# Where the operands of a dense layer lie in on-chip memory, modulo 512 bytes: one gated attention-plus-SiLU kernel, with its buffers moved

## The chip, the cores and the metric

The kernel runs on one core of a Trainium2 chip. The metric is device time in microseconds (us) of one execution; shorter is better. On a core five engines work side by side, each through its own instruction stream: TensorE (PE in the profile, with its weight loads shown as PEld), VectorE (DVE), ScalarE (ACT), GpSimd (POOL) and SyncE (SP), which here issues the DMAs. They meet through semaphores. A matmul on TensorE reads two operands from the on-chip memory SBUF: the stationary one, loaded into the array by a weight load, and the moving one, streamed past it; the result goes to PSUM.

## What is computed

The reference mixes two branches of one input `x` (2048 tokens, 640 features), all in fp32:

```
g = sigmoid((x * gate_w).sum(-1, keepdims=True))
a = attention(x)              # 32 heads of 20; phi = softmax(q w_phi) and softmax(-q w_phi)
                              # o = phi_q (phi_k^T V) / (phi_q phi_k^T 1);  a = o @ wo
b = silu(x @ w1) @ w2         # w1: 640 x 1728, w2: 1728 x 640
out = g * a + (1 - g) * b
```

The attention is linear: `phi_k^T V` is summed over all tokens first, and then each query tile is multiplied by it.

## The kernel before: tiles, stages and names

**Split products.** Every large product is made of three matmuls in a fast fp32 format: an operand is split into a high and a low part (`split`, L117 to L120: ScalarE copies the high part, VectorE or GpSimd subtracts it), and the product takes high x high, high x low and low x high (`PASSES`). So each SBUF tile of an operand holds two halves, `[P, 2, ...]`, and with five chunks of 128 rows one output tile takes 5 x 3 = 15 matmuls.

**Stages**, in TensorE's order:

1. Keys and values (to about 190 us). For 16 token tiles, `kv_proj` (L460) multiplies `x` (tile `xa`, stationary) by the fused weights `wh` and `wl` (moving; a row of 1282 words for each of the five chunks, in pieces of 500, 500 and 282 columns). `kv_acc` (L430) and `kv_rest` (L441) sum `phi_k^T V`.
2. The dense part (to about 580 us). For four blocks of 512 tokens and 13 full tiles and one half tile of the 1728 features: `h_tile` (L507) makes `ph` from a `w1` tile (stationary) and the input tiles `xf` (moving, 512 columns), ScalarE takes the SiLU of it and splits it into a tile `u`; two tiles later `out_acc` (L688) adds `w2` tile (stationary) times `u` (moving, 512 columns) to five accumulators. The first block's first four `w1` products stand in `h_first` (L523).
3. Queries and output (from about 540 us, beside the end of stage 2). `proj` (L418) multiplies `x` (tile `xb` or `xf`, stationary) by `WQ` (moving, two halves of 320 columns), 15 matmuls for each half and 30 for a token tile; `t_mm` (L957) transposes, `n_mm` (L1031) applies `kvw`, and `w_mm` (L1074) applies the output weights `WO` (stationary) to `oT` (moving, 256 columns).

**Where the dense weights lie.** A tile pool lays tiles one behind the other in each partition. The dense weight tiles lie in four kinds of place, which keep their names in the profile:

- `w`, tiles of pool `fq` (`wslot`): the w1 tiles 0 to 4 and w2 tiles 0 to 3. A tile has 1280 words = 5120 bytes = 10 x 512.
- `f`: w2 tile 4, w1 and w2 tiles 5 to 8 and w1 tile 9 (ten tiles) lie as rows inside the two `big` buffers that held `wh` and `wl` before. `big_tile` has rows of `D + 2` = 642 words = 2568 bytes = 5 x 512 + 8, so each of these rows begins 8 bytes further round, modulo 512, than the row before it.
- `w` again, tiles of pool `fp`: w2 tile 9, and w1 and w2 tiles 10 to 12 (seven tiles of 5120 bytes).
- `w_r`: the half tile's weights (`W1R`, `W2R`), in pool `fp` too, with 10 matmuls in place of 15.

`WQ` and `WO` take the two `big` buffers after the `f` tiles. The tiles `xa`, `xf`, `xb` and `u` are slots of 4096 bytes = 8 x 512 (`slot`). The order of all work on each engine is written out by the program (`inorder` and the scheduler behind it).

Of the kernel before, what the change touches and what calls it, by code (L numbers as in the profile page):

```python
# [8 lines left out]
F32 = mybir.dt.float32  # L9
F32R = mybir.dt.float32r  # L10
# [6 lines left out]
P = 128  # L17
S = 2048
D = 640
H = 32  # L20
DH = 20
F = 1728
NC = D // P
NB = S // 512
NT = S // P
# [27 lines left out]
WC = 2 * D + 2  # L53
# [7 lines left out]
def mix_kernel(ctx: ExitStack, tc: tile.TileContext, xT, wqT, wkc, wkr, wv, bd, bdc, cst, wo, w1, w1r, w2, out):  # L61
    nc = tc.nc

    cp = ctx.enter_context(tc.tile_pool(name="cp", bufs=1))
    wp = ctx.enter_context(tc.tile_pool(name="wp", bufs=1))
# [3 lines left out]
    def opened(name, **kw):  # L69
        open_pools[name] = tc.tile_pool(name=name, bufs=1, **kw)  # L70
        return open_pools[name].__enter__()

    def closed(*names):
        for name in names:
            open_pools.pop(name).__exit__(None, None, None)

    fq = opened("fq")
    fu = opened("fu")
    ta = opened("ta")
    psk = opened("psk", space=PSUM)  # L80
    kvp = [psk.tile([P, 512], F32, name=f"kvp{k}") for k in range(3)]
# [14 lines left out]
        return ps.tile([P, 512], F32, tag=f"single{k % 4}", name=name, bufs=1)  # L96

    def raw(name):
        return wp.tile([P, D + 2], F32, tag="raw", name=name, bufs=4)

    def slot(name, pool=None, tag="x", bufs=7):
        return (pool or wp).tile([P, 2, 512], F32R, tag=tag, name=name, bufs=bufs)

    def big_tile(name):
        return wp.tile([P, 2, NC, D + 2], F32R, tag="big", name=name, bufs=2)

    def big(name):
        return big_tile(name).rearrange("p s c d -> p c s d")

    def big_kv(name):  # L110

        return big_tile(name).rearrange("p s c d -> p (s c d)")[:, : NC * WC].rearrange("p (c w) -> p c w", w=WC)

    def wslot(name, dt=F32):
        return fq.tile([P, 2 * D], dt, tag="w", name=name, bufs=NPRE)
# [26 lines left out]

    ident = cp.tile([P, P], F32, name="ident")
    make_identity(nc, ident)
    glog = cp.tile([P, NT], F32, name="glog")
    g = cp.tile([P, NT], F32, name="g")
    g1 = cp.tile([P, NT], F32, name="g1")
    stk = cp.tile([P, 4], F32, name="stk")
    warms = cp.tile([P, 1], F32, name="warms")
    ones = cp.tile([P, P], F32R, name="ones")  # L150
    stage = [ta.tile([P, 2, 2 * D], F32, tag="ph", name=f"stage{k}", bufs=2) for k in range(2)]
    stf = [t.rearrange("p a d -> p (a d)") for t in stage]
    st0 = [t[:, k * D : (k + 1) * D] for t in stf for k in range(3)][:NC]
# [42 lines left out]
    def x_of(t):  # L196
        return [x[:, :, t % 2 * P : (t % 2 + 1) * P] for x in X["t", t // 2]]
# [44 lines left out]
    held = {}  # L242

    def load_f(n):
        w, f = seq[n]
        k = n - NPRE
        if 0 <= k < 10:
            if k % 5 == 0:
                held[k // 5] = big(f"f{k // 5}")
            t = held[k // 5][:, k % 5, :, :D]  # L250
        else:
            t = wslot(f"w{w}_{f}", F32R).rearrange("p (s d) -> p s d", s=2) if n < NPRE else fp.tile([P, 2, D], F32R, name=f"w{w}_{f}")
        r = raw(f"wr{w}_{f}")
        src = w1[f] if w == 1 else w2[f * P : (f + 1) * P, :]
        nc.sync.dma_start(r[:, :D], src)
        split(t[:, 0, :], t[:, 1, :], r[:, :D], "pool" if n < NPRE else "dve")
        W[w, f] = t
# [29 lines left out]
    for k in range(WARM):  # L287
# [5 lines left out]
            stop=(k == WARM - 1),  # L293
        )

    WKV = [big_kv("wh"), big_kv("wl")]
    wh, wl = (w[:, :, :D] for w in WKV)
    LAST = D - NG * GW

# [15 lines left out]
    def kv_share(c, todo):  # L315

        for hx, hw in PASSES:
            for t, lo, hi, opens in todo:
                nc.tensor.matmul(  # L319
                    kv_cols(t, lo, hi),  # L320
                    x_of(t)[c][:, hx, :],
                    WKV[hw][:, c, lo:hi],
                    start=(opens and hx == 0 and hw == 0),
# [8 lines left out]
    def v_weights(c):  # L332
        r = ta.tile([P, 2 * D], F32, tag="e", name="wvr1", bufs=EB)[:, : D + 2] if c == 1 else flat(f"wvr{c}") if c == 2 else raw(f"wvr{c}")
        nc.sync.dma_start(r, wv[c * P : (c + 1) * P, :])
        split(WKV[0][:, c, D:], WKV[1][:, c, D:], r)

# [9 lines left out]
    with inorder(PE, ACT, DVE, POOL):  # L346
# [7 lines left out]
        for lo, hi in ((D, CUTS[2]), (CUTS[2], WC)):  # L354
            split(WKV[0][:, 0, lo:hi], WKV[1][:, 0, lo:hi], wv0[:, lo - D : hi - D])
        cols = [p for pair in zip(values(0), values(1)) for p in pair]
# [99 lines left out]
    def kv_proj(t, lo, hi):  # L456

        xt = x_of(t)
        for n, (hx, hw, c) in enumerate((hx, hw, c) for hx, hw in PASSES for c in range(NC)):
            nc.tensor.matmul(  # L460
                kv_cols(t, lo, hi),
                xt[c][:, hx, :],
                WKV[hw][:, c, lo:hi],
                start=(n == 0),
# [105 lines left out]
    with inorder(ACT, DVE, POOL):  # L570
        for t in range(NT - 1):
# [13 lines left out]
            mm = ta.tile([P, 2, H], F32, tag="mm", name=f"mmk{t}", bufs=2)  # L585
# [21 lines left out]
        t = NT - 1  # L607
# [8 lines left out]
        with inorder(PE):  # L616
# [7 lines left out]
            mm = ta.tile([P, 2, H], F32, tag="mm", name=f"mmk{t}", bufs=2)  # L624
# [48 lines left out]

    closed("psa", "psk", "ta")
    fp = opened("fp", reuse_waits="tile")
    ps = opened("psf", space=PSUM, reuse_waits="tile")

    def bank(name):
# [27 lines left out]
    nc.vector.tensor_tensor(W2R[:FR, 1, :], r[:FR, :D], W2R[:FR, 0, :].bitcast(F32), op=ALU.subtract)  # L706

    def load_wo():
        o = big("wo")
        for c in range(NG):  # L710
            r = raw(f"wo{c}")
            nc.sync.dma_start(r[:GW, :D], wo[c * GW : (c + 1) * GW, :])
            split(o[:GW, c, 0, :D], o[:GW, c, 1, :D], r[:GW, :D])
        return o
# [15 lines left out]
    def q_proj(t):  # L730
# [8 lines left out]
        for j in range(2):  # L739
            proj(dst[j], xq(t), WQ, j * HALF, HALF)  # L740
        return parts
# [2 lines left out]

    def q_open(t, parts):
        sm = fu.tile([P, 8 * H], F32, tag="sm", name=f"sm{t}", bufs=3)
        mm = fu.tile([P, 2, H], F32, tag="mmq", name=f"mmq{t}", bufs=2)
        sums.setdefault(t, sm[:, : 2 * H])
        e = wslot(f"eq{t}")
        Q[t] = {  # L750
            "e": e,
            "sm": sm,
            "mv": mm.rearrange("p i (a h) -> p i a h", a=2),
            "ev": e.rearrange("p (a h s f) -> p a h s f", a=2, s=2, f=DH),
            "parts": [(part, slice(k * 2 // len(parts), (k + 1) * 2 // len(parts))) for k, part in enumerate(parts)],
        }
# [121 lines left out]
    for b in range(NB):  # L878
        order = ORDERS[b]
        if b + 1 < NB:  # L880
            load_x("f", b + 1)
        acc = [bank(f"acc{b}_{m}") for m in range(NC)]
        us = {} if b else us0
        for n, f in enumerate(order):
            if f not in us:
                us[f] = h_tile(b, f)
            if n == 4:
                if b == 0:
                    pg = bank("pg")
                    nc.tensor.transpose(pg[:NT, :P], g1, ident)  # L890
                    gT = fp.tile([NT, P], F32, name="gT")
                    nc.scalar.copy(gT, pg[:NT, :P])
                    nc.sync.dma_start(g_d, gT)
                G1 = fp.tile([P, 512], F32, tag="G1", name=f"G1_{b}", bufs=1)
                nc.sync.dma_start(
                    G1, g_d.rearrange("t p -> (t p)")[b * 512 : (b + 1) * 512].partition_broadcast(P)
                )
            if n > 1 and n < NF:
                for m in range(NC):
                    out_acc(order, order[n - 2], us[order[n - 2]], acc, m)  # L900
            if b < NB - 1:
                continue
            if n == 2:
                load_b_consts()
            if n == 5:
                WQ = big("wq")
                zbc = wslot("zbc")
                nc.sync.dma_start(zbc, kv_d[KF].partition_broadcast(P))
            if 5 <= n < 5 + GR:
                gi = n - 5  # L910
                rq = raw(f"wTq{gi}")
                load_fused(gi, rq[:, :D])
                for c0, c1 in ((0, 4), (4, NC)):
                    fused(kvb["bd"], WQ[:, :, 0, :], WQ[:, :, 1, :], gi, rq, bank(f"pwq{gi}_{c0}"), c0, c1)
            if n == 8:
                WO = load_wo()
            if n == 9:
                kvw = [wslot(f"kvw{h}", F32R)[:GW, : 2 * NG * GW].rearrange("p (j f) -> p j f", f=GW) for h in range(2)]
                kvwr = fu.tile([RC, 2, GW], F32R, name="kvwr")
                make_kvw()  # L920
            if n == 8:
                xb_load(0)
                xb_split(0)
                xb_load(1)
                xb_split(1)
                xb_load(2)
            if 10 <= n < NF:
                t = 2 * NP - 4 + n - 10
                q_tile(t)
                if n < NF - 1:  # L930
                    q_rest(t)

        def acc_mm(m):
            for f in order[-3:]:
                out_acc(order, f, us[f], acc, m)

        def acc_out(m):
            o = fp.tile([P, 512], F32, tag="o", name=f"o{b}_{m}", bufs=2)
            nc.vector.tensor_tensor(o, acc[m], G1, op=ALU.mult)
            nc.sync.dma_start(fb_d[m, :, b * 512 : (b + 1) * 512], o)  # L940

        if b < NB - 1:
            for m in range(NC):
                acc_mm(m)
                acc_out(m)
# [33 lines left out]
    t = 2 * NP - 1  # L979
# [33 lines left out]
    tb = opened("tb", reuse_waits="tile")  # L1013
# [266 lines left out]
    with inorder(PE, DVE, ACT, POOL):  # L1280
# [15 lines left out]
        for u in range(1, NP - 2):  # L1296
            step(u)
        last_steps(NP - 2)
    closed("psb", "tb", "fu", "fq")


# [63 lines left out]
```

## Time and profile before

| what | value |
|---|---|
| median of 3 runs | 763.94 us (763.82 to 764.4) |
| span of the profiled execution | 764.0 us |
| TensorE busy | 758.5 us, 99% of the span |
| TensorE clock granted | 1.000 |
| VectorE, ScalarE, GpSimd busy | 370.4, 267.5 and 263.2 us |
| dense part on TensorE: `w`, `f`, `w_r` | 223.6, 141.5 and 19.8 us |

The profile lists the instructions of one execution. Consecutive matmuls overlap, so the duration shown for one (about 390 ns for 512 columns) is longer than the step from one start to the next. That step is what a matmul costs when TensorE is the bound. It is read from the start times in the timeline: a group of 15 that starts at A, and whose successor starts at B without a wait, costs B - A. The chain of work that ended last shows the same: the time of a group in it is the group's share of the path.

### The profile page before, as it was taken

Reading aid. Unit: us, or ns where it says so; the run is one execution under the profiler, and the core shown is the slowest. Engines: PE = TensorE matmul, PEld = TensorE weight load, DVE = VectorE, ACT = ScalarE, POOL = GpSimd, SP = SyncE. Lnnn points to the kernel's source line nnn. Section 1 sums busy time; section 2 is a strip of 40 time slices with the busy share of each in tenths; the row PEclk is TensorE's granted clock in tenths of the full one; section 3 lists DMA queues with packets and bytes.
Section 4 is the critical chain, followed back from the end, with each engine's and each line's share of the span. In section 5 each row is a group of like instructions: output and inputs, shape, how many; then the busy total and the mean of one; then the engine's idle time right before and its main releaser. Section 6 shows DMA issues by size and latency. Waiting matters only on the chain.

```text
span 764.0 us, 10659 instructions
## 1 busy us (share of the span) xinstructions
PE 758.5 (99%) x4259; PEld 668.0 (87%) x4259; DVE 370.4 (48%) x662; ACT 267.5 (35%) x484; POOL 263.2 (34%) x163
## 2 busy tenths in 40 slices
PE   8999999999999999999999999999999999999998
PEld 7888888888888888888888888888899999999998
DVE  4677666676651221012211122122587888787861
ACT  4454443346542311122111222133554543424341
POOL 2398777767100000000000000001166766855551
PEclk9999999999999999999999999999999999999999
DMA  7111111103660120002200015022004232111222
GB/s 247 59 53 52 53 52 53 59 31 101 190 189 1 59 93 1 1 0 72 84 0 1 1 48 179 4 74 90 15 1 142 80 96 77 49 56 43 70 70 91
DMA packets 35454, 50.36 MB, mean 66 GB/s; under 512 B 3539, under 2 KB 23267, under 8 KB 35405
## 3 DMA queue, kind: packets, MB, share of 16 engines
q1 hardware_dynamic: 35117, 49.18, 20.6%
q8 instruction: 33, 0.54, 0.3%
q10 hardware_dynamic: 288, 0.51, 0.3%
q14 instruction: 16, 0.13, 0.1%
HBM read 38.56 MB, written 11.11 MB: 65 GB/s over the span
## 4 chain that ended last, share of the span: by engine, by line
PE 97%; DVE 1%; DMA 1%; ACT 0%; POOL 0%; issue 0%; SPq 0%; POOLq 0%; DVEq 0%; ACTq 0%
PE acc L688 25%; PE ph L507 23%; PE kvp L460 16%; PE pq L418 9%; PE pa L1074 9%; PE pn L1031 4%; PE kv L430 2%; PE pT L957 2%; PE kvp L523 2%; PE kvp L319 1%; PE kvq L319 1%; PE pwk L308 1%; PE pwq L228 1%; DMA wvr<-wv 1%; POOL eq L817 0%; PE pkvt L862 0%
## 5 line engine op out<-in xcount | busy, mean ns | idle before, releaser
L120 POOL TENSOR_TENSOR xb<-xrb,xb 128x512 fp32r<-128x512 f32 (+1 forms) x18 | 19.8, 1120 | 341.4 <-ACT xb L118 341.4
L120 DVE TENSOR_TENSOR u<-ph,u 128x512 fp32r<-128x512 f32 x48 | 33.2, 691 | 178.0 <-ACT u L118 177.9
L688 PE MATMUL acc<-u,w 128*128 128x512 f32 x480 | 114.7, 392 | 0.0
L688 PEld LDWEIGHTS acc<-u,w 128*128 128x128 f32 x480 | 89.5, 188 | 19.1 <-ACT u L118 0.3
L507 PE MATMUL ph<-xf,w 128*128 128x512 f32 x420 | 99.8, 390 | 0.0
L509 ACT ACTIVATE ph<-ph 128x512 f32<-128x512 f32 x48 | 27.9, 582 | 189.0 <-PE ph L507 189.0
L507 PEld LDWEIGHTS ph<-xf,w 128*128 128x128 f32 x420 | 78.7, 188 | 16.6
L460 PE MATMUL kvp<-wh,xa 128*128 128x500 f32 (+1 forms) x420 | 93.0, 357 | 0.0
L460 PEld LDWEIGHTS kvp<-wh,xa 128*128 128x128 f32 x420 | 71.6, 188 | 9.8
L1074 PE MATMUL pa<-oT,wo 120*128 120x256 f32 x600 | 76.8, 282 | 0.0
L1074 PEld LDWEIGHTS pa<-oT,wo 120*128 120x128 f32 x600 | 73.7, 188 | 0.0
L688 PE MATMUL acc<-u,f 128*128 128x512 f32 x300 | 73.3, 394 | 0.0
L507 PE MATMUL ph<-xf,f 128*128 128x512 f32 x300 | 72.7, 394 | 0.0
L507 PEld LDWEIGHTS ph<-xf,f 128*128 128x128 f32 x300 | 56.4, 188 | 13.1
L688 PEld LDWEIGHTS acc<-u,f 128*128 128x128 f32 x300 | 56.2, 188 | 13.0
L781 POOL TENSOR_TENSOR ez<-eq,zbc 128x1280 f32<-128x1280 f32 x16 | 48.1, 3009 | 39.3 <-ACT eq L767 39.2
L120 POOL TENSOR_TENSOR ph<-ek,ph 128x1280 fp32r<-128x1280 f32 x16 | 47.6, 2972 | 27.8 <-ACT ph L118 27.8
L418 PE MATMUL pq<-wq,xb 128*128 128x320 f32 x360 | 55.5, 311 | 0.0
L418 PEld LDWEIGHTS pq<-wq,xb 128*128 128x128 f32 x360 | 53.1, 188 | 0.0
L460 PE MATMUL kvp<-wl,xa 128*128 128x500 f32 (+1 forms) x210 | 47.4, 356 | 0.0
L817 POOL TENSOR_TENSOR eq<-eq,sm 128x1280 f32<-128x1280 f32 x16 | 37.9, 2369 | 15.0 <-DVE sm L811 13.9
L488 POOL TENSOR_TENSOR ek<-ek,st 128x1280 f32<-128x1280 f32 x16 | 38.0, 2375 | 9.1 <-issue 6.1
(159 smaller groups left out, 1108.9 us busy)
## 6 DMA issues: line engine op xcount, KB each, us to landing
wr<-w SPq DMA_DIRECT2D x26, 320.0 KB, 3.5
xrf<-xT SPq DMA_DIRECT2D x20, 256.0 KB, 3.7
fb_d<-o SPq DMA_DIRECT2D x20, 256.0 KB, 2.3
y<-fb_d SPq DMA_DIRECT2D x16, 256.0 KB, 2.9
out<-y SPq DMA_DIRECT2D x16, 256.0 KB, 2.3
xra<-xT SPq DMA_DIRECT2D x14, 256.0 KB, 2.6
xrb<-xT SPq DMA_DIRECT2D x12, 256.0 KB, 2.8
xra<-xT SPq DMA_DIRECT2D x12, 128.0 KB, 2.8
```

The source lines that it names most:

```text
L120: eng.tensor_tensor(lo, src, hi.bitcast(F32), op=ALU.subtract)
L319: nc.tensor.matmul(kv_cols(t, lo, hi), x_of(t)[c][:, hx, :], WKV[hw][:, c, lo:hi], start=(opens and hx == 0 and hw == 0), stop=(c == NC - ...
L418: nc.tensor.matmul(dst, xt[c][:, hx, :], w[:, c, hw, lo : lo + n], start=first, stop=(hx == 1 and c == NC - 1))
L460: nc.tensor.matmul(kv_cols(t, lo, hi), xt[c][:, hx, :], WKV[hw][:, c, lo:hi], start=(n == 0), stop=(n == 3 * NC - 1), skip_group_check=True,)
L488: nc.gpsimd.tensor_tensor(groups(e), groups(e), spread(st[:, 1, :]), op=ALU.mult)
L507: nc.tensor.matmul(ph, lhs, rhs, start=(n == 0), stop=(n == len(todo) - 1))
L509: nc.scalar.activation(hs, ph, AF.Silu)
L688: nc.tensor.matmul(acc[m], lhs, rhs, start=(f == order[0] and n == 0), stop=(f == order[-1] and n == len(todo) - 1))
L781: nc.gpsimd.tensor_tensor(ez, Q[t]["e"], zbc, op=ALU.mult)
L817: nc.gpsimd.tensor_tensor(groups(q["e"]), groups(q["e"]), spread(q["sm"][:, 2 * H : 4 * H]), op=ALU.mult)
L1031: nc.tensor.matmul(pns[u, gp][:GW, a, :], kvw_of(hk, 2 * i + jj)[:w], f[:w, hp, jj * 256 : (jj + 1) * 256], start=(n == 0), stop=(n == 3 * ...
L1074: nc.tensor.matmul(pa[:, a, :], WO[:GW, c, hw, ds] if c < NG else WOR[:, ds], o[:, ho, c, :], start=(k == 0), stop=(k == len(todo) - 1),)
```

## The change

No instruction is added, removed or moved. Row for row, each of the five engines has the same operations on the same named tiles in the same order, and each waits for the same events, but for one pair of neighbouring copies of ScalarE that name their two DMA queues in the other order. What differs is where tiles lie:

- The `raw` staging buffers (642 words) go from the pool `wp` to a pool of their own, `rawp`, behind `fu`.
- `ones` goes ahead; `g`, `g1`, `stk`, `warms` and the softmax extremes `mmq` go between the large buffers, with some fillers (`gap0` to `gap4`) that nothing uses or that a later tile takes.
- The two `big` buffers become two tags (`big0`, `big1`), one buffer each, of 5 x 1282 words. `f`, `WQ` and `WO` lie in them with rows of 640 words = 2560 bytes = 5 x 512. `wh` and `wl` keep rows of 1282 words. Each tenant follows the same one as before.

```
-    def big_tile(name):
-        return wp.tile([P, 2, NC, D + 2], F32R, tag="big", name=name, bufs=2)
-
-    def big(name):
-        return big_tile(name).rearrange("p s c d -> p c s d")
+    def extremes(name, home):
+        return wp.tile([P, 2, H], F32, tag=f"mmq{home}", name=name, bufs=1)
+
+    def big_tile(name, home):
+        return wp.tile([P, NC * WC], F32R, tag=f"big{home}", name=name, bufs=1)
+
+    def big(name, home):
+        t = big_tile(name, home)[:, : 2 * NC * D]
+        return t.rearrange("p (s c d) -> p c s d", s=2, d=D)
...
+    wh_t = big_tile("wh", 0)
+    g = wp.tile([P, NT], F32, name="g")
...
+    wl_t = big_tile("wl", 1)
+    extremes("gap1", 1)
+    wp.tile([P, 48], F32, name="gap2")
+    slot("gap3")
...
     fp = opened("fp", reuse_waits="tile")
+    fp.tile([P, 112], F32, name="gap4")
```

The start of each operand as the two programs are built, in bytes modulo 512 (c is the chunk, 0 to 4):

| product | moving: before, now | stationary: before, now |
|---|---|---|
| dense, `w` in `fq` | `xf`, `u`: 192, 192 | 192, 192 |
| dense, `f` | `xf`, `u`: 192, 192 | eight-byte steps: 384 to 416 (`f1`) and 480 to 0 (`f0`) for the high halves, 40 more for the low; now 192 |
| dense, `w` in `fp` and `w_r` | `xf`, `u`: 192, 192 | 128, 192 |
| queries, first 320 columns | `WQ`: 480 to 40 in steps of 8; 192 | `xb`, `xf`: 192, 192 |
| queries, last 320 columns | `WQ`: 224 to 296 in steps of 8; 448 | `xb`, `xf`: 192, 192 |
| output | `oT`: 128, 256 | `WO`: 384 to 456 in steps of 8; 192 |
| keys and values | `wh` from 384 + 8c, `wl` from 480 + 8c; both from 192 + 8c | `xa`: 192, 192 |
| key-value sums | `ph` from 128; from 256 | `v` from 128 or 384; from 256 or 0 |

More of the change, by code (lines that the diff above doesn't have):

```diff
@@ L78, in mix_kernel @@
     fu = opened("fu")
+    rawp = opened("rawp")
     ta = opened("ta")
@@ L98, in raw @@
     def raw(name):
-        return wp.tile([P, D + 2], F32, tag="raw", name=name, bufs=4)
+        return rawp.tile([P, D + 2], F32, tag="raw", name=name, bufs=4)
     def slot(name, pool=None, tag="x", bufs=7):
         return (pool or wp).tile([P, 2, 512], F32R, tag=tag, name=name, bufs=bufs)
-    def big_tile(name):
-        return wp.tile([P, 2, NC, D + 2], F32R, tag="big", name=name, bufs=2)
-    def big(name):
-        return big_tile(name).rearrange("p s c d -> p c s d")
-    def big_kv(name):
-        return big_tile(name).rearrange("p s c d -> p (s c d)")[:, : NC * WC].rearrange("p (c w) -> p c w", w=WC)
+    def extremes(name, home):
[5 more added lines that the diff above has]
+        return t.rearrange("p (s c d) -> p c s d", s=2, d=D)
     def wslot(name, dt=F32):
@@ L144, in mix_kernel @@
     make_identity(nc, ident)
+    ones = cp.tile([P, P], F32R, name="ones")
     glog = cp.tile([P, NT], F32, name="glog")
[L146 to L150, printed above, removed]
+    wh_t = big_tile("wh", 0)
+    g = wp.tile([P, NT], F32, name="g")
+    g1 = wp.tile([P, NT], F32, name="g1")
+    stk = wp.tile([P, 4], F32, name="stk")
+    extremes("gap0", 0)
+    warms = wp.tile([P, 1], F32, name="warms")
+    wl_t = big_tile("wl", 1)
+    extremes("gap1", 1)
+    wp.tile([P, 48], F32, name="gap2")
+    slot("gap3")
     stage = [ta.tile([P, 2, 2 * D], F32, tag="ph", name=f"stage{k}", bufs=2) for k in range(2)]
@@ L248, in load_f @@
             if k % 5 == 0:
-                held[k // 5] = big(f"f{k // 5}")
+                held[k // 5] = big(f"f{k // 5}", 1 - k // 5)
             t = held[k // 5][:, k % 5, :, :D]
@@ L294, in mix_kernel @@
         )
-    WKV = [big_kv("wh"), big_kv("wl")]
+    WKV = [t.rearrange("p (c w) -> p c w", w=WC) for t in (wh_t, wl_t)]
     wh, wl = (w[:, :, :D] for w in WKV)
@@ L708, in load_wo @@
     def load_wo():
-        o = big("wo")
+        o = big("wo", 0)
         for c in range(NG):
@@ L746, in q_open @@
         sm = fu.tile([P, 8 * H], F32, tag="sm", name=f"sm{t}", bufs=3)
-        mm = fu.tile([P, 2, H], F32, tag="mmq", name=f"mmq{t}", bufs=2)
+        mm = extremes(f"mmq{t}", t % 2)
         sums.setdefault(t, sm[:, : 2 * H])
@@ L905, in mix_kernel @@
             if n == 5:
-                WQ = big("wq")
+                WQ = big("wq", 1)
                 zbc = wslot("zbc")
@@ L1298, in mix_kernel @@
         last_steps(NP - 2)
-    closed("psb", "tb", "fu", "fq")
+    closed("psb", "tb", "rawp", "fu", "fq")
 def kernel(A_x, A_wqkv, A_w_phi, A_wo, B_x, B_w1, B_w2, gate_w):
```

## The prediction, made before the changed kernel was run

> **What bounds the kernel now.** I read the page first, for the engine that carries the span: the span, busy shares, the clock, and the chain of work that ended last.
>
> ```profile
> span 764.0 us, 10659 instructions
> ...
> PE 758.5 (99%) x4259; PEld 668.0 (87%) x4259; DVE 370.4 (48%) x662; ACT 267.5 (35%) x484; POOL 263.2 (34%) x163
> ...
> PEclk9999999999999999999999999999999999999999
> ...
> PE 97%; DVE 1%; DMA 1%; ACT 0%; POOL 0%; issue 0%; SPq 0%; POOLq 0%; DVEq 0%; ACTq 0%
> ```
>
> TensorE is busy for 99% of the span, and 97% of the chain is its own work. Hardly anything is waited for, so time can only come out of the step from one matmul's start to the next. The profiled span, 764.0, is within 0.1 us of the median of the three runs, 763.94; sums made on the trace go straight onto the median.
>
> The second view is the windows by stage (window, length, then busy time of PE, PEld, DVE, ACT, POOL):
>
> ```profile
> 190.00:535.00 345.00, 345.00 (x1542) 283.47 (x1541) 82.11 (x125) 88.82 (x155) 5.77 (x7) 1.00 0.20 61
> 535.00:764.00 229.00, 225.40 (x1688) 219.32 (x1686) 165.44 (x279) 92.06 (x163) 128.84 (x81) 1.00 0.21 66
> ```
>
> In the dense stage TensorE has no gap at all in 345 us, and in the last stage 3.6 us of 229. The other engines have slack in both.
>
> The third view decides the case: TensorE's timeline in the dense part's second block (start, length, group of equal matmuls). The length holds the tail that overlaps the next group, so a group's cost is the next row's start minus its own.
>
> ```profile
> 291.90 3.56 PE L507 MATMUL ph<-xf,w 128*128 128x512 f32 x15
> 295.30 3.56 PE L688 MATMUL acc<-u,w 128*128 128x512 f32 x15
> 298.70 3.59 PE L507 MATMUL ph<-xf,f 128*128 128x512 f32 x15
> 302.13 3.57 PE L688 MATMUL acc<-u,w 128*128 128x512 f32 x15
> 305.54 3.66 PE L507 MATMUL ph<-xf,f 128*128 128x512 f32 x15
> 309.04 3.63 PE L688 MATMUL acc<-u,f 128*128 128x512 f32 x15
> 312.51 3.62 PE L507 MATMUL ph<-xf,f 128*128 128x512 f32 x15
> 315.97 3.63 PE L688 MATMUL acc<-u,f 128*128 128x512 f32 x15
> 319.44 3.66 PE L507 MATMUL ph<-xf,f 128*128 128x512 f32 x15
> 322.94 3.66 PE L688 MATMUL acc<-u,f 128*128 128x512 f32 x15
> 326.43 2.46 PE L507 MATMUL ph<-xf,w_r 128*128 128x512 f32 x10
> 328.73 3.64 PE L688 MATMUL acc<-u,f 128*128 128x512 f32 x15
> 332.21 3.65 PE L507 MATMUL ph<-xf,f 128*128 128x512 f32 x15
> 335.70 3.63 PE L688 MATMUL acc<-u,f 128*128 128x512 f32 x15
> 339.17 3.60 PE L507 MATMUL ph<-xf,w 128*128 128x512 f32 x15
> 342.60 2.45 PE L688 MATMUL acc<-u,w_r 128*128 128x512 f32 x10
> 344.89 3.60 PE L507 MATMUL ph<-xf,w 128*128 128x512 f32 x15
> 348.33 3.60 PE L688 MATMUL acc<-u,w 128*128 128x512 f32 x15
> 351.76 3.60 PE L507 MATMUL ph<-xf,w 128*128 128x512 f32 x15
> 355.19 1.07 PE L688 MATMUL acc<-u,w 128*128 128x512 f32 x4
> ```
>
> All these rows are the same work: 512 columns against 128 x 128 weights. Yet a group on a `w` tile of pool `fq`, whose weights begin at 192 modulo 512 like the moving operand, takes 3.40 us (291.90 to 295.30 to 298.70). The groups on `f`, whose rows move on by 8 bytes, take 3.43 to 3.50, and those on the `w` tiles of pool `fp`, at 128, take 3.43 or 3.44. The kind of product (L507 or L688) makes no difference, and no group waits. What goes with the step is where the stationary operand lies against the moving one.
>
> **The change part by part.** It adds and removes no instruction; each engine's order and its waits stay. So every term is a number of matmuls times a change of step, and all of it lies on the path.
>
> *Dense, `f`.* The ten `f` groups of this block cost 3.43 (298.70 to 302.13), 20.89 for six (305.54 to 326.43) and 10.44 for three (328.73 to 339.17): 34.76 together. At the 3.40 of a `w` group they cost 34.00, which is 0.76 less. How many blocks have them:
>
> ```profile
> L688 PE MATMUL acc<-u,f 128*128 128x512 f32 x300 | 73.3, 394 | 0.0
> L507 PE MATMUL ph<-xf,f 128*128 128x512 f32 x300 | 72.7, 394 | 0.0
> ```
>
> 600 matmuls are 40 groups, four blocks of ten: 3.0 us.
>
> *Dense, `w` in `fp`, and `w_r`.* Four `fp` groups cost 3.43 (339.17 to 342.60) and 10.30 for three (344.89 to 355.19): 13.73, or 0.033 each above 3.40. Seven groups in four blocks are 28: 0.9 us. The two `w_r` groups of ten matmuls cost 2.30 and 2.29 against 10/15 of 3.40 = 2.27: 0.06 a block, 0.2 us. The dense part gives 3.0 + 0.9 + 0.2 = 4.1 us.
>
> [...]
>
> *Does the gain arrive?* It does if the weights and the SiLU tiles are ready that much sooner. The `f` tiles' users and makers (count, ns of one, first and last start):
>
> ```profile
> L507 PE MATMUL ph<-xf,f x300: 388/394/401, 204.7 to 499.4; 128*128 128x512 f32 x150
> ...
> L120 DVE TENSOR_TENSOR f<-wr,f x10: 816/825/828, 193.3 to 207.8; 128x640 fp32r<-128x640 f32 x10
> ```
>
> And the wait behind these products (us in total, times, longest):
>
> ```profile
> ACT ph L509 <- PE ph L507: 189.0, 37, 11.9
> ```
>
> VectorE is done with all ten tiles at 208.6, while the first is used at 204.7 and the rest over the next 40 us, in which TensorE gains under 1 us. ScalarE sits 189 us waiting for `ph`: it follows TensorE. Were that cover gone, a group would wait for its tile, at most the 0.1 us it had gained.
>
> *Queries, output, keys and values.* The change moves these operands too. Their groups in the chain (start, length on the path, group):
>
> ```profile
> 104.65 6.79 PE kvp L460 x30
> 111.67 1.97 PE kvp L460 x15
> ...
> 609.77 5.65 PE pa L1074 x48
> ...
> 617.45 4.43 PE pq L418 x30
> ```
>
> Per column the aligned dense group costs 3.40/(15 x 512) = 0.443 ns, its worst neighbour (3.50) 0.456. Queries cost 4.43/(30 x 320) = 0.461, output 5.65/(48 x 256) = 0.460, the long key pieces 6.79/(30 x 500) = 0.453, the short ones 1.97/(15 x 282) = 0.466, the dearest clean rate here.
>
> Queries, first half: `WQ` comes to 192, where `x` is, for all 15 matmuls; this is the dense part's case. At 0.443 a half costs 2.13 in place of 2.21, and the 16 token tiles have one each: 1.4 us. Bounds 0 and 1.4; I take 1.4, for the dense rows are the same operation with the same relation.
>
> Queries, second half: `WQ` at 448 against 192, a distance that no row shows. Bounds: -1.4, and +0.4 at 0.466. I take 0.
>
> Output: `oT` at 256 against `WO` at 192, where steps of 8 bytes were before. At 0.443 the 48 would cost 5.44, and the code's 640 of them (8 token pairs x 5 x 16) are 13.3 such groups: -2.8; at 0.466, +0.9. The distance of 64 is that of the `fp` rows (0.447), with the roles the other way round; for 256 columns no row shows a gain, so I take 0.
>
> Keys and values: chunks keep their 8-byte steps and only begin elsewhere. For 16 token tiles the bounds are -4.0 (6.64 and 1.87 a tile, at 0.443) and +3.1 (6.99 for the long pieces at 0.466). I take 0: one set of scattered distances replaces another. In the key-value sums both operands move by 128 bytes, so their distance stays: 0.
>
> Sum: 763.94 - 4.1 - 1.4 = 758.4 us.
>
> **The rivals.**
>
> *Dense part only:* the relation counts for nothing at 320 columns. 763.94 - 4.1 = 759.8. For it: queries run at 0.461, dearer than any dense group, so something else may be in it.
>
> *All rows on one grid gain:* the second query half and the output too, -1.4 and -2.8 beyond the forecast: 754.2. For it: before, all of these were off the 64-byte grid; against it: 256 columns show no such thing yet.
>
> *Half the cure:* the 3.40 belongs to pool `fq` for another reason, and `f` comes only to the 3.43 of the `fp` rows. Ten groups at 3.43 are 34.3, 0.46 less a block: 1.8 us, 762.1. Against it: `fp` and `fq` tiles have one shape and differ in place alone.
>
> *The place is not the cause:* it goes with something else, such as what runs beside. Then 763.9. Against it: the six `f` groups of 305.54 to 326.43 lie between `w` groups of 3.40 and 3.43 with nothing else changing, and `w` groups of both products agree. [...]
>
> *Slower:* scattered operands pay for the cure. If meeting at one place is good only for pieces of the full 512 columns and bad for shorter ones, the products of 256 to 500 columns rise by the spread that the dense rows show, 3.50/3.40 or 2.9%. They hold 16 x (6.79 + 1.97 + 4.43) + 13.3 x 5.65 = 286 us: +8.4, less 4.1: 768.2. It decides from a rise of 4.1/286 = 1.4%, and ends clearly slower from 2.0%. Against it: these groups are at or near the dearest rates already.
>
> **How the numbers follow.** Forecast 0.47, dense only 0.26, all gain 0.08, half the cure 0.07, place not the cause 0.08, slower 0.04. The time is the forecast's, 758.4. The range takes in the forecast, dense only and half the cure (0.80), so up to 762.1; downward it goes to 756.5, some two thirds of the output's 2.8. The likeliest case alone would span 757 to 760. About 0.2%, 1.5 us, is what a measurement of this kernel can tell from no change: the forecast, dense only, all gain and half the cure lie beyond it on the fast side (0.88), place not the cause within it (0.08), the last beyond it on the slow side (0.04).
>
> **What would show each step.** Right: every dense group of 15 takes 3.40 in the timeline of the changed kernel, on `f` too, and `w_r` groups 2.27; the query groups of 30 take 4.34 in the chain, output 5.65, keys 6.79. Wrong: `f` groups still differ among themselves (place not the cause), stay at 3.43 (half the cure), or the gain stands in the groups but a wait of TensorE gives it back; or the key and output groups move by more than 1%, so that what I set at 0 decides the sum.

## The result and the profile after

The changed kernel takes 758.84 us, the median of 5 runs (758.59 to 761.28), against 763.82 of the kernel before in 5 runs (763.56 to 764.4): a ratio of 0.994, with a 95% interval of 0.9928 to 0.9952. The forecast was 758.4, its range 756.5 to 762.1.

The page of the changed kernel, with the same parts as were shown of before:

```profile
span 759.5 us, 10659 instructions
...
PE 754.0 (99%) x4259; PEld 667.6 (88%) x4259; DVE 370.6 (49%) x662; ACT 267.6 (35%) x484; POOL 262.3 (35%) x163
```

The span fell by 4.5 us and TensorE's busy time by the same 4.5, from 758.5 to 754.0. Its idle time stayed at 5.5. So no waiting went away: matmuls became shorter.

TensorE's timeline of the changed kernel in the dense part's second block (start, length, group); a group's cost is the next start minus its own:

```profile
297.36 3.56 PE L514 MATMUL ph<-xf,f 128*128 128x512 f32 x15
300.76 3.56 PE L696 MATMUL acc<-u,w 128*128 128x512 f32 x15
304.16 3.56 PE L514 MATMUL ph<-xf,f 128*128 128x512 f32 x15
...
324.56 2.43 PE L514 MATMUL ph<-xf,w_r 128*128 128x512 f32 x10
326.83 3.56 PE L696 MATMUL acc<-u,f 128*128 128x512 f32 x15
...
337.03 3.56 PE L514 MATMUL ph<-xf,w 128*128 128x512 f32 x15
340.43 2.43 PE L696 MATMUL acc<-u,w_r 128*128 128x512 f32 x10
342.69 3.56 PE L514 MATMUL ph<-xf,w 128*128 128x512 f32 x15
```

Where before the `f` groups cost 3.43 to 3.50 and the late `w` groups 3.43, every group of 15 in this block now costs 3.40, and a `w_r` group of ten 2.26 or 2.27. The lengths are all 3.56, where they were 3.56 to 3.66.

The groups of before that the prediction did not show, by product (count, then busy us and mean ns):

```profile
L688 PE MATMUL acc<-u,w 128*128 128x512 f32 x480 | 114.7, 392 | 0.0
L507 PE MATMUL ph<-xf,w 128*128 128x512 f32 x420 | 99.8, 390 | 0.0
L460 PE MATMUL kvp<-wh,xa 128*128 128x500 f32 (+1 forms) x420 | 93.0, 357 | 0.0
L1074 PE MATMUL pa<-oT,wo 120*128 120x256 f32 x600 | 76.8, 282 | 0.0
```

And those of the changed kernel:

```profile
L696 PE MATMUL acc<-u,w 128*128 128x512 f32 x480 | 114.4, 391 | 0.2 <-ACT u L119 0.2
L514 PE MATMUL ph<-xf,w 128*128 128x512 f32 x420 | 99.4, 389 | 0.0
L467 PE MATMUL kvp<-wh,xa 128*128 128x500 f32 (+1 forms) x420 | 92.6, 356 | 0.0
L1082 PE MATMUL pa<-oT,wo 120*128 120x256 f32 x600 | 76.4, 280 | 0.0
L696 PE MATMUL acc<-u,f 128*128 128x512 f32 x300 | 71.8, 390 | 0.0
L514 PE MATMUL ph<-xf,f 128*128 128x512 f32 x300 | 71.3, 389 | 0.0
```

`f` went from 73.3 + 72.7 to 71.8 + 71.3: -2.9. `w` gave -0.7, keys with `wh` -0.4, output -0.4. The dense part is most of it. The first row of the changed kernel also shows a wait of 0.2 us for a `u` tile, which the row of before does not have.

In the chain of waits of the changed kernel (start, length on the path, group), the rows that answer to those of before:

```profile
34.46 8.79 PE kvp L467 x45
...
104.66 6.76 PE kvp L467 x30
...
605.70 5.59 PE pa L1082 x48
...
613.28 4.40 PE pq L425 x30
```

Keys went from 6.79 to 6.76, output from 5.65 to 5.59, queries from 4.43 to 4.40. Of the query groups of before, the 4.43 is the dearest but one; most rows of that chain show 4.42, and most of the changed kernel 4.40. For 16 token tiles 0.02 is 0.3 us, and the busy time agrees: 55.5 + 18.4 us before, 55.3 + 18.3 now. The first row is for the start-up, which comes back with the last experiment.

### The profile page after: what moved, and what is told of

It is laid out like the page before. It is cut to its first block, busy times and chain, and to the rows that moved or that the text cites. A ratio compares the mean times of both kernels' runs of the same rounds, so it can differ in the third digit from the quotient of the medians.

```text
span 759.5 us, 10659 instructions
## 1 busy us (share of the span) xinstructions
PE 754.0 (99%) x4259; PEld 667.6 (88%) x4259; DVE 370.6 (49%) x662; ACT 267.6 (35%) x484; POOL 262.3 (35%) x163
## 4 chain that ended last, share of the span: by engine, by line
PE 95%; DMA 2%; DVE 1%; ACT 1%; POOL 0%; issue 0%; SPq 0%; POOLq 0%; DVEq 0%; ACTq 0%
PE acc L696 24%; PE ph L514 22%; PE kvp L467 16%; PE pq L425 9%; PE pa L1082 9%; PE pn L1039 4%; PE kv L437 2%; PE pT L965 2%; PE kvp L530 2%; PE kvp L326 1%; PE kvq L326 1%; PE pwk L315 1%; DMA wvr<-wv 1%; DMA wo<-wo 1%; PE pwq L235 0%; DMA xrb<-xT 0%
## 5 line engine op out<-in xcount | busy, mean ns | idle before, releaser
L1082 PE MATMUL pa<-oT,wo 120*128 120x256 f32 x600 | 76.4, 280 | 0.0
L1082 PEld LDWEIGHTS pa<-oT,wo 120*128 120x128 f32 x600 | 73.3, 188 | 0.0
L696 PE MATMUL acc<-u,f 128*128 128x512 f32 x300 | 71.8, 390 | 0.0
L514 PE MATMUL ph<-xf,f 128*128 128x512 f32 x300 | 71.3, 389 | 0.0
L425 PE MATMUL pq<-wq,xb 128*128 128x320 f32 x360 | 55.3, 310 | 0.0
```

The source lines that it names most:

```text
L425: nc.tensor.matmul(dst, xt[c][:, hx, :], w[:, c, hw, lo : lo + n], start=first, stop=(hx == 1 and c == NC - 1))
L514: nc.tensor.matmul(ph, lhs, rhs, start=(n == 0), stop=(n == len(todo) - 1))
L696: nc.tensor.matmul(acc[m], lhs, rhs, start=(f == order[0] and n == 0), stop=(f == order[-1] and n == len(todo) - 1))
L1082: nc.tensor.matmul(pa[:, a, :], WO[:GW, c, hw, ds] if c < NG else WOR[:, ds], o[:, ho, c, :], start=(k == 0), stop=(k == len(todo) - 1),)
```

## The experiments

The theory: in a run of 512-column matmuls the step depends on how far the stationary operand lies from the moving one, modulo some period. The rivals were that the absolute place counts (192, or a multiple of 64), and that the pool, the neighbours or something else sets the step. "Distance" below is the stationary operand's start minus the moving one's, modulo 512 bytes.

### Rows of `f` back to 642 words, all else as changed

Two small tiles also change place or size, so that all else stays where it is:

```
-    def big(name, home):
-        t = big_tile(name, home)[:, : 2 * NC * D]
+    def big(name, home, d=D):
+        t = big_tile(name, home)[:, : 2 * NC * d]
...
-                held[k // 5] = big(f"f{k // 5}", 1 - k // 5)
+                held[k // 5] = big(f"f{k // 5}", 1 - k // 5, D + 2)
```

> The changed kernel, with rows of 642 words (2568 bytes) for the f tiles alone; WQ and WO keep rows of 640, all other tiles stay at 192 modulo 512. Theory (the step depends on where the weights begin against the moving operand): the f groups of 15 go back from 3.40 us to 3.43 to 3.50, different from tile to tile, the w groups stay at 3.40, and the kernel takes 2 to 3.5 us more than the changed one (758.84). Rival (the place is not the cause, the gain came from elsewhere in the new layout): f groups stay at 3.40, 758.8 us.

Measured: 761.88 us, a ratio to before of 0.9979 (0.9971 to 0.9988). Timeline of this kernel in the second block:

```profile
295.97 3.64 PE L513 MATMUL ph<-xf,f 128*128 128x512 f32 x15
299.45 3.60 PE L696 MATMUL acc<-u,w 128*128 128x512 f32 x15
302.89 3.63 PE L513 MATMUL ph<-xf,f 128*128 128x512 f32 x15
306.35 3.64 PE L696 MATMUL acc<-u,f 128*128 128x512 f32 x15
```

The `f` groups cost 3.48 and 3.46 again (295.97 to 299.45, 302.89 to 306.35). The loss against the changed kernel is 761.88 - 758.84 = 3.0 us, the size of the `f` term. A `w` tile between two of them costs 3.44, where it costs 3.40 in the changed kernel (300.76 to 304.16), so a group is touched by its neighbours too. The distances of these `f` tiles run from 0 to 72 in steps of 8: lying near the moving operand is not enough for 3.40.

### The late `w` tiles back to 128

```
-    fp.tile([P, 112], F32, name="gap4")
+    fp.tile([P, 96], F32, name="gap4")
```

> The changed kernel, with the filler ahead of the late weight tiles (pool fp: seven w tiles and w_r) 64 bytes shorter, so that they begin at 128 and the moving operand at 192, as before the change. Theory: their groups go from 3.40 back to 3.43 us and the two groups of ten from 2.27 to 2.30, f stays at 3.40; 1.0 us more than the changed kernel. [...]

Measured: 759.73 us, 0.9949 (0.9936 to 0.9963). The timeline, where `f` ends and the late `w` begins:

```profile
332.08 3.56 PE L696 MATMUL acc<-u,f 128*128 128x512 f32 x15
335.48 3.60 PE L514 MATMUL ph<-xf,w 128*128 128x512 f32 x15
338.91 2.45 PE L696 MATMUL acc<-u,w_r 128*128 128x512 f32 x10
341.20 3.60 PE L514 MATMUL ph<-xf,w 128*128 128x512 f32 x15
```

`f` 3.40, `w` 3.43, `w_r` 2.29. The steps agree with the prediction's 0.9 + 0.2; of the time itself, 0.9 us above the changed kernel, the intervals of the two ratios overlap, so the steps carry this verdict.

### Everything 32 bytes further

```
+    cp.tile([P, 8], F32, name="shift")
```

> The changed kernel, with every tile moved by 32 bytes: all dense operands begin at 224 modulo 512, none on a multiple of 64, and every distance between two operands is as it was. Theory (the distance counts): all dense groups stay at 3.40 us, 758.8 us. Rival (the absolute place counts, a multiple of 64 or 192 itself): all 105 full dense groups pay 0.03 to 0.10 us more, 762 to 768 us.

Measured: 758.3 us, 0.9932 (0.9919 to 0.9944). All dense operands begin at 224 now, which is no multiple of 64:

```profile
294.83 3.56 PE L515 MATMUL ph<-xf,f 128*128 128x512 f32 x15
298.24 3.56 PE L697 MATMUL acc<-u,w 128*128 128x512 f32 x15
301.63 3.56 PE L515 MATMUL ph<-xf,f 128*128 128x512 f32 x15
```

The groups cost 3.41 and 3.39, and the time is not above the changed kernel's. Neither 192 itself nor a multiple of 64 is needed.

### A sweep: each `w` tile 32 bytes further than the one before

```
-PAB = 2
+PAB = 1
...
-        return fq.tile([P, 2 * D], dt, tag="w", ...)
+        return fq.tile([P, 2 * D + 8], dt, tag="w", ...)[:, : 2 * D]
```

(the `fp` tiles likewise). `xf` and `f` stay at 192; `u` falls on 480.

> The changed kernel with the w tiles 5152 bytes apart in place of 5120, so that each lies 32 bytes further round modulo 512 (u moves to 480 with them; f stays at 192; one buffer less for a copy of the last stage). It measures the step against the distance from the moving to the stationary operand. Theory: a group's step follows from that distance alone; 0 gives 3.40 in both products, wherever it lies, f costs 3.40 against xf (distance 0) and more against u (distance 224), and the dear distances reach 3.50. Rival (absolute place): f costs 3.40 against u too.

Measured: 769.25 us in one run, slower than before the change. Timeline:

```profile
295.11 3.67 PE L696 MATMUL acc<-u,w 128*128 128x512 f32 x15
298.62 3.62 PE L514 MATMUL ph<-xf,f 128*128 128x512 f32 x15
302.08 3.60 PE L696 MATMUL acc<-u,w 128*128 128x512 f32 x15
305.51 3.59 PE L514 MATMUL ph<-xf,f 128*128 128x512 f32 x15
308.94 3.66 PE L696 MATMUL acc<-u,f 128*128 128x512 f32 x15
312.44 3.59 PE L514 MATMUL ph<-xf,f 128*128 128x512 f32 x15
...
348.32 3.61 PE L696 MATMUL acc<-u,w 128*128 128x512 f32 x15
351.77 3.61 PE L514 MATMUL ph<-xf,w 128*128 128x512 f32 x15
355.21 7.12 PE L696 MATMUL acc<-u,w 128*128 128x512 f32 x30
...
362.40 3.61 PE L696 MATMUL acc<-u,w 128*128 128x512 f32 x15
```

The `f` tiles all begin at 192. Those that meet `xf` (distance 0) cost 3.46 and 3.43, those that meet `u` cost 3.50 (308.94 to 312.44; distance 224): it is the pair that counts, not the place of the weights alone. The `w` tile that starts at 302.08 is at distance 256 and costs 3.43; the one that starts at 295.11, at 352, costs 3.51. Those at 351.77 and 362.40 (to 365.85) are at 448 and 192: 3.44 and 3.45. The one at 348.32, the first of pool `fp`, is at distance 0 and yet costs 3.45. It comes behind a dear group, as does the one at 302.08: by their starts the first seven or eight matmuls of both take 224 to 236 ns each, the next six 226 or 227, as in the groups of 3.40. The distances 64, 96, 320, 384, 416 and 480 cost 3.48 to 3.51 where one has a group to itself. At 160, inside a row of 44 equal matmuls, each takes 233 ns, or 3.50 for 15. The least clear is 128, which only stands in the 30 at 355.21, behind 64: 6.95 for both. So 0 and 256 pair, and 192 and 448 pair, which fits a period of 256; the next run tests 256 on groups in a row. Part of the 10 us is not dense: the output groups of 48, with `oT` at another place too and one buffer less for what becomes of them, take 5.73 in its chain.

### `f` at distance 40 and the late `w` at 256

```
-    def big(name, home):
-        t = big_tile(name, home)[:, : 2 * NC * D]
+    def big(name, home, at=0):
+        t = big_tile(name, home)[:, at : at + 2 * NC * D]
...
-                held[k // 5] = big(f"f{k // 5}", 1 - k // 5)
+                held[k // 5] = big(f"f{k // 5}", 1 - k // 5, 10)
...
-    fp.tile([P, 112], F32, name="gap4")
+    fp.tile([P, 48], F32, name="gap4")
```

> The changed kernel, with the f tiles 40 bytes further on (at 232 modulo 512, distance 40 from the moving operand) and the late w tiles and w_r at 448 (distance 256). In the runs so far the distance 40 cost as little as 0 in the few matmuls that had it, and 256 as little as 0 in the sweep, while 64, 96 and 320 cost 0.10 us a group. Theory now (what counts is the distance modulo 256, and 40 is as good as 0): f and late w groups take 3.40 us, 758.8 us. Rival (only one place modulo 512 is good): f groups 3.43 to 3.50 and late w groups 3.43 or more, 761 to 764 us.

Measured: 758.47 us, 0.9934 (0.9922 to 0.9947). Timeline:

```profile
294.78 3.56 PE L514 MATMUL ph<-xf,f 128*128 128x512 f32 x15
298.18 3.56 PE L696 MATMUL acc<-u,w 128*128 128x512 f32 x15
...
334.44 3.56 PE L514 MATMUL ph<-xf,w 128*128 128x512 f32 x15
337.84 2.43 PE L696 MATMUL acc<-u,w_r 128*128 128x512 f32 x10
```

Both cost 3.40 (294.78 to 298.18, 334.44 to 337.84). One place modulo 512 is enough but not needed: 256 apart is as good, and so are 40 bytes.

### The inputs alone at distance 96

```
+    fq.tile([P, 24], F32, name="gap5")
...
-    wp.tile([P, 48], F32, name="gap2")
+    wp.tile([P, 24], F32, name="gap2")
```

The inputs go 96 bytes back, to 96 modulo 512; the dense weights and `u` stay together at 192.

> The changed kernel, with the input tiles alone (xa, xf, xb) 96 bytes lower, at 96 modulo 512, a distance that cost 3.50 us in the sweep; weights and u stay at 192. Theory: the 13 products with w1 in each block go to 3.50 us a group, 52 groups less none, 5.2 us, the second product stays at 3.40; about 764 us, no faster than the kernel before the change though all dense tiles lie on multiples of 32 and all weights at one place. Rival (the weights' place alone counts): 758.8 us.

Measured: 765.71 us, 1.0028 (1.0017 to 1.0039): slower than before the change, from moving the inputs alone. Timeline:

```profile
297.44 3.67 PE L515 MATMUL ph<-xf,f 128*128 128x512 f32 x15
300.95 3.58 PE L697 MATMUL acc<-u,w 128*128 128x512 f32 x15
304.37 3.67 PE L515 MATMUL ph<-xf,f 128*128 128x512 f32 x15
```

The products with the input cost 3.51, their neighbours, which kept their distance of 0, 3.42. A pair of such groups costs 6.93 in place of 6.80. For 13 pairs in each of four blocks that is 6.8 us, an estimate, where 6.9 us above the changed kernel were measured. The query group of 30 is 4.41 in the chain of waits, against 4.40. Its two halves are at distances 0 and 256 in the changed kernel and at 416 and 160 here. At 512 columns the first two cost 3.40 and the last two 3.50; at 320 columns the difference is 0.01 for 30 matmuls.

The output groups rise too, although neither `oT` nor `WO` has moved (0.4 us of busy time in all). A group of 48 in the chain, 5.59 in the changed kernel:

```profile
609.83 5.66 PE pa L1083 x48
```

TensorE's timeline shows where. In the changed kernel the first 15 of such a group, right behind a query group, take 1.71 us (605.53 to 607.24) and the next 15 take 1.77 (607.36 to 609.13). With the inputs moved the first 15 take 1.78 (609.66 to 611.44), and before the change they took 1.77 (609.60 to 611.37). So 5.59 or 5.66 does not follow from the output's own distance, which is 448 in both. The inputs moved, and the query group just ahead reads them: that a group is touched by the one before it fits, as in the dense part, but no run separates it.

### Output: `WO` at distance 0 from `oT`

```
-        o = big("wo", 0)
+        o = big("wo", 0, 16)
...
-                kvw = [wslot(...)[:GW, : 2 * NG * GW].rearrange("p (j f) -> p j f", f=GW) ...]
+                kvw = [wslot(...)[:GW].rearrange("p (j f) -> p j f", f=P)[:, :, :GW] ...]
```

> The changed kernel, with WO 64 bytes further on, at 256 modulo 512 where oT lies, and the rows of kvw 512 bytes apart in place of 480, so that all of them begin at 192 (fT at 192 or 256). It asks whether products of 256 columns gain from the distance 0. Theory (0 is the best distance at every length): output groups of 48 fall from 5.63 us in the chain by 0.1 or more and the kernel by 1 to 3 us. Rival (short pieces hide it, as the 320 columns of the queries did): within 0.3 us of 758.8.

Measured: 759.93 us, 0.9951 (0.9937 to 0.9964). In the chain of waits:

```profile
603.01 5.75 PE pa L1082 x48
```

A miss: the kernel is 1.1 us above the changed one, the output became dearer, 5.75 against 5.59, and its `wo` products rose from 76.4 to 78.0 us of busy time:

```profile
L1082 PE MATMUL pa<-oT,wo 120*128 120x256 f32 x600 | 78.0, 284 | 0.0
```

For 256 columns the distance that is best at 512 is the dearest tried: 5.75 at 0, against 5.59 or 5.66 at 448, 5.65 scattered before, and 5.73 in the sweep (160). It shows behind other output groups too: the second 15 of this group take 1.80 us (604.75 to 606.55), where at 448 they take 1.77 with and without the inputs moved.

### Keys and values on one grid

The 500-column pieces of `wh` and `wl` were laid out in rows of 1024 words, the first pieces at distance 0 and the second at 40:

```
+WP = 1024
+WP1 = 502
...
-                WKV[hw][:, c, lo:hi],
+                wcols(hw, c, lo, hi),
```

> The changed kernel, with the key and value weights laid out so that every 500-column piece begins at 192 or at 152 modulo 512 (distance 0 or 40) from xa at 192, for which 18 small copies are added at the start, and some small tiles change places. Theory (long pieces pay for the distance): a pair of 500-column pieces (30 matmuls) falls from 6.78 us to 6.65, the 282-column pieces stay, 2 us less in all, 756.5 to 757.5 us if the added copies cost up to 1 us. Rival (only the 512-column products are sensitive): 758.8 us or more.

Measured: 759.4 us, 0.9944 (0.9931 to 0.9958). In the chain:

```profile
112.92 6.79 PE kvp L476 x30
```

A miss again: 6.79, no better than the changed kernel's 6.76. That 500 columns are close to 512 was my reason; it does not hold. Splits of the weights were added for this layout, and they may cost a little of the start.

### Keys at 240, output at 56

The same layout four words on, and `WO` 30 words on. These were the distances at which single matmuls of 500 and 256 columns looked cheapest in the traces with mixed rows. In the trace of the changed kernel the average step from one 500-column matmul to the next is 222 ns at 240 and 223 at 24, against 226 over all distances, 224 at 0 and 228 at 40. In the trace of before the median step of 256 columns is 114 ns at 48 and at 56, against 118 over all; by the average only 48 is cheap, 115.6 ns, and 56 takes 117.8, as all do together. A cycle of the expectation is the 0.417 ns that a column takes by the estimate in the next section.

```
+        return (wh_t, wl_t)[hw][:, at + 4 : at + 4 + hi - lo]
...
+        o = big("wo", 0, 30)
```

> The previous layout of the key and value weights, moved on by 16 bytes: the 500-column pieces stand at the distances 240 and 24 (modulo 256) from xa, which were the cheap ones for 500 columns where rows of all distances came by in the traces so far (34 and 37 cycles over the column count, against 42 on average and 39 and 46 at the distances 0 and 40); and WO at 56 from oT, the cheapest distance that 256 columns had (21 against 26). Theory (each length has good distances of its own, and they hold when every matmul has them): pairs of 500-column pieces fall from 6.8 to 6.7 us, output groups from 5.63 to 5.55 us in the chain, 756 to 757.5 us in all, the best so far. Rival (those cheap matmuls were cheap through their neighbours in a row of changing distances, not by themselves): within 0.6 us of 758.8 or slower.

Measured: 758.78 us, 0.9939 (0.9927 to 0.9952), against 758.58 for the changed kernel in the same series. In the chain:

```profile
111.84 6.75 PE kvp L476 x30
...
602.60 5.67 PE pa L1091 x48
```

A miss as well: keys 6.75, no gain to speak of against 6.76; output 5.67, no better than the 5.66 that 448 can cost. A distance at which single matmuls looked cheap between others of other distances (222 ns at 240) is not cheap for a row of equals (6.75/30 = 225). That their neighbours had made them cheap fits, but no run separates it.

### The changed kernel once more

> The changed kernel itself once more, beside the runs of this call, for a second profile: its first one had a slower start (the first 30 us) than those of the experiments. All theories: 758.3 to 759.1 us, dense groups of 15 at 3.40 us, span about 757 us.

Measured: 758.58 us, 0.9938 (0.9924 to 0.9951). Its chain:

```profile
32.45 8.79 PE kvp L467 x45
```

The profiled execution took 758.74 us and spanned 757.0; that of the result took 761.28 and spanned 759.5. The same group of keys starts at 32.45 here and at 34.46 there, so these 2 us lie in the start-up, which differs from execution to execution. Later groups keep them, and the wait for a `u` tile, which only the first of the two profiles has, adds 0.5 (the output group of 48 starts at 603.18 and 605.70). Before the change it started at 34.37:

```profile
34.37 8.75 PE kvp L460 x45
```

So the two profiles, before and after, are both of slow starts and may be set against each other.

No version beat the changed kernel clearly: 758.3 and 758.47 (32 bytes further; `f` at 40) have intervals that overlap with its own.

## Why the prediction was right, point by point

- **TensorE's own step is the bound:** right. Its busy time and the span fell by the same 4.5 us.
- **Dense, `f`, -3.0:** right; -2.9 in the groups, and 3.0 us lost again when its rows went back.
- **Late `w` and `w_r`, -0.9 and -0.2:** right in the steps (3.43 to 3.40, 2.30 to 2.27). The busy time of all `w` groups fell by 0.7 us in the first profile, which has the extra wait, and by 1.2 in the second (114.0 and 99.3 us).
- **Queries, first half, -1.4:** this step failed. I carried the saving per column from 512 columns to 320. The group of 30 went to 4.40, not 4.34: 0.3 us in place of 1.4. By the period of 256 the second half, at distance 256, stands as well as the first, so even two good halves bring no more. The prediction's own rates were there to warn me, since they rose as the pieces got shorter (0.443 ns a column at 512, 0.453 at 500, 0.461 at 320, 0.466 at 282). In the changed kernel 512 columns cost 3.40/15 = 227 ns and 320 cost 4.40/30 = 147, so the 192 columns between them cost 80 ns, 0.417 each, and some 13 ns remain for each matmul. That is an estimate from two lengths; by the same 0.417, 256 columns (5.59/48) leave 10 ns and 500 (6.76/30) leave 17. The 0.461 of the queries was mostly such a part spread over fewer columns, not a bad place.
- **Output and keys, 0:** mis-sized by -0.4 each (`wo` and `wh`), within their bounds; the output's part lay in the 15 matmuls behind a query group and went again when the inputs alone were moved, which no term had. The products with `kvw`, which the sum does not have either, took 0.3 more (35.4 + 4.1 to 35.6 + 4.2). With the queries' -0.3 this gives -0.8, where the forecast had -1.4. So that the total came within 0.5 us is partly luck: errors cancelled. The rival "dense part only", at 759.8, had the reason right for the queries and missed the output and the keys.
- **The sum against the median:** I took the profiled span, 764.0, for the time. In these runs an execution takes about 1.8 us more than its span (758.74 and 757.0), so the profiled execution of before took about 765.8, an estimate, and had a slow start. No term depends on it, since the difference was laid on the median.
- **Rivals.** *Half the cure* and *the place is not the cause* fell with the 3.40 of every group and with the sweep. There `f` tiles at one place cost 3.43 with one partner and 3.50 with the other. *All rows on one grid gain* fell with the query groups, 4.40 with both halves at good distances, and with the output at distance 0, 5.75. *Slower* did not come from the shorter pieces of this change, but what it feared can happen: the output does pay when it is put where 512 columns like it (5.75 at distance 0, against 5.59).
- **What stays open.** Why the distance matters: the runs show that it does, 3.40 at 0, 40 and 256 and 3.50 at 224, and not what makes it so. Where between 320 and 512 columns the effect begins is open too, since 500 columns did not follow (6.79 at 0 and 40, 6.76 scattered) and lengths between were not tried. So is why the output behind a query group changes its step when its own operands stay (1.71 to 1.78 us for 15).

## What to carry to other kernels

When TensorE is busy 99% of the span, compare the steps of equal groups before anything else: the same product at 3.40 and at 3.50 us is a finding, and its cause may lie in the addresses of a pair of operands, not in an instruction. Lay the operands of long matmuls so that each pair keeps a distance that has been measured as good (here 0, 40 or 256 bytes modulo 512, with 3.40 us for 15 matmuls of 512 columns), and look at every product that shares an operand, since moving the inputs by 96 bytes cost 6.9 us. Do not scale such a gain to other lengths (a query group of 30 fell from 4.43 to 4.40, not to 4.34); take the fixed part off first (here some 13 ns a matmul, an estimate), and measure each length by itself.

## What was not expected of the hardware

- At 512 columns the step follows the distance of the two operands, as if with a period of 256 bytes: 3.40 at 0, 40 and 256, 3.43 to 3.45 at 192 and 448, 3.48 to 3.51 at nearly every other distance tried.
- At 320 columns almost no dependence shows (4.40 with the halves at 0 and 256, 4.41 at 416 and 160, mostly 4.42 scattered), and at 256 columns distance 0 is dear (5.75 against 5.59 or 5.66 at 448).
- A group's neighbours count: groups at distance 0 between groups at 96 cost 3.42, not 3.40, and 15 output matmuls at one and the same distance take 1.71 or 1.78 us behind a query group, with the inputs at 192 or at 96.
- The first 34 us of an execution vary by 2 us with no change in the program: the same group of keys starts at 32.45 and at 34.46 us.
